# Sorting V as rows in four array tiles, by way of DRAM, for two of four batches of a block-sorted attention with a squared-ReLU MLP

## The chip, the cores and the metric

The kernel runs on one core of one Trainium2 chip. The metric is the device time of one execution in microseconds (us); the profiler's span is the time from the first to the last instruction of the profiled execution.

## The reference

Four batches, eight heads, 768 positions in eight blocks of 96, 64 features per head. A small 8x8 matrix per head, made nearly doubly stochastic by five rounds of normalisation, mixes whole blocks of K and V; each block of Q then attends to one mixed block. The result goes through two dense layers with a squared ReLU between.

```python
P = sort_net                                    # (B, H, 8, 8)
for _ in range(5):
    P = P - np.max(P, axis=-1, keepdims=True)
    P = np.exp(P)
    P = P / (np.sum(P, axis=-1, keepdims=True) + 1e-09)
    P = P / (np.sum(P, axis=-2, keepdims=True) + 1e-09)
k_sorted = np.einsum('bhij,bhjcd->bhicd', P, k_b)
v_sorted = np.einsum('bhij,bhjcd->bhicd', P, v_b)
scores = scale * np.matmul(q_b, k_sb.transpose(0, 1, 2, 4, 3))
attn = softmax(scores)
x = np.matmul(attn, v_sb)                       # -> (3072 tokens, 512)
h = x @ w_in                                    # 512 -> 2048
g = s * np.maximum(h, 0.0) ** 2 + b
out = g @ w_out                                 # 2048 -> 512
```

## The kernel before

All matmuls take bf16 and accumulate in fp32 in PSUM. Work is staged by batch, and each batch by halves of four blocks (384 tokens). The order on every engine is written out by hand: `ffn1` (first dense layer) and `ffn2` (second) each take a dictionary of slots, and pieces of the next batch's attention are called at these slots, between the dense layer's matmuls. So TensorE (PE) works through one fixed list, in order, and waits at whatever comes next on it.

`ffn1` goes over eight pairs of 128 hidden features; ScalarE (ACT) applies the ReLU to a pair and VectorE (DVE) squares it into `gt`. `ffn2` goes over three tiles of 128 tokens with sixteen matmuls each, and its slots count groups of four matmuls. Attention for batch n runs in the two `ffn2` of batch n-1:

- K pieces (`k_piece`, L247): raw K with (head, block, half) in the partitions is the stationary operand, the mixing matrix `PD` the moving one. This sorts K and at once turns it so that features lie in the partitions (`KS`).
- V pieces (`v_piece`, L298): the same with V, but sorted V (`VS`) needs positions in the partitions. So raw V is first permuted by feature into `VP` (GpSimd, POOL, L171, eight copies a batch), and then each of 64 features gets two matmuls of 64 columns: 128 matmuls a batch in four pieces of 32. Each piece is evacuated by ACT or DVE.
- scores with an exponential on ACT (`s_piece`), then P pieces (`p_piece`, L352) that multiply the exponentials with `VS`, whose extra columns of ones give the sums, and a normalisation on DVE.
- the attention result is transposed by DMA (`t_dma`), as Q is (`q_dma`), on the SyncE (SP) queue, which also carries the output stores.

POOL loads K, V and Q by casting DMAs. For batch 1 they follow the weights' loads and some memsets; for batches 2 and 3 they are held back by a gate until the first square of `ffn1` of the batch before them. Raw tiles have two buffers (`rawp`), `VP`, `KS` and `VS` have two each. PSUM has two pools: `psa`, three buffers of two banks, used by `ffn1`, K, V, scores and P; `psb`, two buffers of one bank, used by `ffn2`. Batch 0's attention runs at the start and is not changed but for the name of its mask.

Of the kernel before, what the change touches and what calls it, by code (L numbers as in the profile page):

```python
# [16 lines left out]
def spread(t, dims):  # L17

    return bass.AP(tensor=t.tensor, offset=t.offset, ap=[list(t.ap[0])] + dims)
# [3 lines left out]
def kernel(  # L23
# [26 lines left out]
    KR = GAP + C2  # L50
    NG = NHP * NB
    VW = D + 2
    CK = 16
    scale = float(D) ** -0.5


    raw = [t.rearrange("b h (j z c) d -> b (h j z) (c d)", j=NB, z=2) for t in (q, k, v)]

    const = ctx.enter_context(tc.tile_pool(name="const", bufs=1))
    rawp = ctx.enter_context(tc.tile_pool(name="rawp", bufs=2))  # L60
    trp = ctx.enter_context(tc.tile_pool(name="trp", bufs=2))
    atp = ctx.enter_context(tc.tile_pool(name="atp", bufs=6))
    xp = ctx.enter_context(tc.tile_pool(name="xp", bufs=2))
# [3 lines left out]
    osb = ctx.enter_context(tc.tile_pool(name="osb", bufs=3))  # L67
    psa = ctx.enter_context(tc.tile_pool(name="psa", bufs=3, space=bass.MemoryType.PSUM))
    psb = ctx.enter_context(tc.tile_pool(name="psb", bufs=2, space=bass.MemoryType.PSUM))
    ctx.enter_context(tc.manual_schedule())  # L70


# [11 lines left out]
    def load(t, b, parts=1):  # L84
        ti = rawp.tile([128, C2, D], BF, tag=f"raw{t}", name=f"raw{t}")
        RAW[t, b] = ti
        n = C2 // parts
        for c in range(0, C2, n):
            nc.gpsimd.dma_start(out=ti[:, c:c + n, :].rearrange("p c d -> p (c d)"),
                                in_=raw["qkv".index(t)][b][:, c * D:(c + n) * D])  # L90

    QTOK = {}

    def load_q(b, ns=range(NB)):
# [4 lines left out]
        for n in ns:  # L99
# [2 lines left out]
    zeros = const.tile([128, 512], BF)  # L102
    nc.vector.memset(zeros[:, 0:128], 0.0)  # L103
    nc.vector.memset(zeros[:, 128:512], 0.0)  # L104
    VP = [const.tile([128, D, GAP], BF, name=f"vp{i}") for i in range(2)]
    KS = [const.tile([128, NG, 2, GAP], BF, name=f"ks{i}") for i in range(2)]
    VS = [const.tile([KR, 2 * NG, VW], BF, name=f"vs{i}") for i in range(2)]
    nc.vector.memset(VP[0][:, :, C2:GAP], 0.0)
    nc.vector.memset(KS[0][:, :, :, C2:GAP], 0.0)
    nc.vector.memset(sne[:, NB, :], 1e-9)  # L110

# [3 lines left out]
    idv = ident.rearrange("p (a e j z) -> p a e j z", a=NHP, e=2, j=NB)  # L115
    emat = const.tile([BH, B, 128], FP)
    nc.gpsimd.memset(emat, 0.0)
    nc.gpsimd.affine_select(out=emat, in_=emat, pattern=[[-H, B], [-1, H], [0, 2 * NB]], base=0,
                            channel_multiplier=1, compare_op=ALU.not_equal, fill=1.0)
    load("k", 0, 3)  # L120
    load_q(0, range(HB))
# [24 lines left out]
            fs = slice(c * (NF // 4), (c + 1) * (NF // 4))  # L146
            nc.gpsimd.dma_start(out=wo[:, fs, :], in_=wov[:, fs, :])

    def fill_vs(i):
        nc.gpsimd.memset(VS[i][:, :, D:VW], 1.0)  # L150
        nc.gpsimd.memset(VS[i][32:GAP, :, D:VW], 0.0)
        nc.gpsimd.memset(VS[i][32:C2, :, D:VW], 1.0)

    fill_vs(0)
    Z = []

    def warm(n, w=512):
# [4 lines left out]
                             start=True, stop=True)  # L162


    def permute(eng, b, src, cs=slice(0, C2), ds=slice(0, D)):
        o = VP[b % 2][:, ds, cs]
        i = src[:, cs, ds].rearrange("p c d -> p d c")
        if eng is nc.scalar:
            eng.copy(out=o, in_=i)
        else:  # L170
            eng.tensor_copy(out=o, in_=i)  # L171
# [3 lines left out]
    rrec = const.tile([BH, NB], FP)  # L175
    jsel = const.tile([128, NB], FP)
    bm = const.tile([128, 2 * 2 * NHP], FP)
    idle = [
        lambda: nc.vector.tensor_reduce(
            out=jsel, in_=ident.rearrange("p (h j z) -> p j h z", h=H, j=NB), axis=AX.XY, op=ALU.add),  # L180
# [8 lines left out]
    for it in range(5):  # L189
        nc.scalar.activation(out=sn, in_=sn, func=AF.Exp)  # L190
        if it >= 1:
            permute(nc.scalar, 0, v0f, slice((it - 1) * CV, it * CV))
        if it in (1, 2):
            idle[it - 1]()
        nc.vector.tensor_reduce(out=rstat, in_=sn, axis=AX.X, op=ALU.add)
        nc.vector.reciprocal(out=rrec, in_=rstat)
        nc.vector.tensor_tensor(out=sn, in0=sn, in1=rrec.broadcast_to([BH, NB, NB]), op=ALU.mult)
        if it == 4:
            break
        nc.vector.tensor_reduce(out=rstat, in_=sne.rearrange("p i j -> p j i"),  # L200
                                axis=AX.X, op=ALU.add)
        nc.vector.reciprocal(out=rrec, in_=rstat)
        nc.vector.tensor_tensor(out=sn, in0=sn, in1=spread(rrec, [[0, NB], list(rrec.ap[1])]),
                                op=ALU.mult)
# [11 lines left out]
                             rhs=sn.rearrange("p i j -> p (i j)"), start=True, stop=True)  # L216
        return pe

    def take_p(b0, n, pe):

        bs = slice(b0, b0 + n)
        tmp = rtp.tile([128, n * NB, NB], FP, tag=f"tmp{n}", name="tmp")
        nc.vector.tensor_tensor(out=tmp, in0=pe.rearrange("p b i j -> p (b i) j"),
                                in1=spread(jsel, [[0, n * NB], list(jsel.ap[1])]), op=ALU.mult)
        nc.vector.tensor_reduce(out=PT[:, bs].rearrange("p b i -> p (b i)"), in_=tmp, axis=AX.X,
                                op=ALU.add)
        cs = rtp.tile([128, n], FP, tag=f"cs{n}", name="cs")
        nc.vector.tensor_reduce(out=cs, in_=PT[:, bs], axis=AX.X, op=ALU.add)
        nc.vector.reciprocal(out=RC[:, bs], in_=cs)

    def build_pd(b):
        pd = const.tile([128, 2, 2, NG], BF, name=f"pd{b}")
        nc.vector.scalar_tensor_tensor(
            out=pd.rearrange("p e z (a i) -> p (e z a) i", i=NB),
            in0=spread(bm, [list(bm.ap[1]), [0, NB]]), scalar=RC[:, b:b + 1],
            in1=spread(PT[:, b], [[0, 4 * NHP], list(PT.ap[2])]), op0=ALU.mult, op1=ALU.mult)
        PD[b] = pd

    def evac(eng, out, in_):
        if eng == "A":  # L240
            nc.scalar.copy(out=out, in_=in_)  # L241
        else:
            nc.vector.tensor_copy(out=out, in_=in_)  # L243
# [47 lines left out]
    def q_dma(b):  # L291
        qt = q_tile(b)
        for n0 in (0, HB):
            nc.sync.dma_start_transpose(
                out=qt[:, n0:n0 + HB].rearrange("p n a t -> p (n a) t"),
                in_=QTOK[b][:, n0:n0 + HB].rearrange("p n h d -> p (n h d)"))

    def v_piece(b, d0, eng):  # L298
        ps = psa.tile([128, CK, 2 * NG], FP, tag="a", name="tv")
        for d in range(CK):  # L300
            for z in range(2):
                nc.tensor.matmul(out=ps[z * GAP:(z + 1) * GAP, d, :],  # L302
                                 lhsT=VP[b % 2][:, d0 + d, :], rhs=PD[b][:, :, z, :],
                                 start=True, stop=True)
        evac(eng, VS[b % 2][:, :, d0:d0 + CK], ps[0:KR].rearrange("p d g -> p g d"))

    AT = {}
    X = {}
# [32 lines left out]
    def p_piece(b, half, hp, later=False):  # L341
# [6 lines left out]
        for e in range(2):  # L348
            for n in range(HB):
                c0 = (e * HB + n) * BLK  # L350
                m = 128 if c0 + 128 <= 2 * TG else BLK
                nc.tensor.matmul(out=pv[0:m, e, n * VW:(n + 1) * VW],  # L352
                                 lhsT=atf[:, c0:c0 + m], rhs=VS[b % 2][:, e * NG + g0 + n, :],
                                 start=True, stop=True)

        def norm():
# [100 lines left out]
        nc.sync.dma_start(out=out[r0:r0 + 128, ns], in_=ot[:, ns])  # L457


    take_p(0, 1, spread_p(0, 1))  # L460
    build_pd(0)

    nc.gpsimd.tensor_copy(out=ones[:, 0:1], in_=PD[0][:, 0, 0, 0:1])
# [31 lines left out]
    nc.gpsimd.memset(sel, 0.0)  # L495
    for r in range(0, 128, 32):
        nc.gpsimd.memset(sel[r:r + 1], 1.0)
    nc.gpsimd.memset(VP[1][:, :, C2:GAP], 0.0)
    nc.gpsimd.memset(KS[1][:, :, :, C2:GAP], 0.0)
    fill_vs(1)  # L500
    for t, src in ((s_bc, moe_s), (b_bc, moe_b)):
        nc.gpsimd.dma_start(out=t, in_=src.to_broadcast([128, 1]))

    def v_sort(b):
        for i in range(8):
            permute(nc.gpsimd, b, RAW["v", b], ds=slice(i * 8, (i + 1) * 8))

    def loads(b):
        load("k", b)
        load("v", b)  # L510
        load_q(b)
        v_sort(b)

    loads(1)

# [20 lines left out]

    def K(b, i, eng): return lambda: k_piece(b, i * CK, eng)
    def V(b, i, eng): return lambda: v_piece(b, i * CK, eng)
    def SC(b, h, i): return lambda: s_piece(b, h, i)
    def SB(b, h, i): return lambda: s_banks(b, h, i)  # L540
    def P(b, h, i): return lambda: p_piece(b, h, i)
# [2 lines left out]
    def PDB(b): return lambda: build_pd(b)  # L544
    def QB(b, n0, eng): return lambda: q_blocks(b, n0, eng)
# [2 lines left out]
    ffn1(0, {-1: [TP(0, 0, 2, "AD")], ("pre", 1): [QB(0, HB, "D"), QB(0, HB + 2, "D")],  # L548
             2: [SB(0, 1, 0)], 3: [SB(0, 1, 1), P(0, 1, 0)], 4: [SB(0, 1, 2), P(0, 1, 1)],
             5: [SB(0, 1, 3), P(0, 1, 2)], 6: [TP(0, 1, 0, "D"), P(0, 1, 3)]}, ahead=3)  # L550
    ffn1(1, {-2: [TP(0, 1, 2, "D")], 1: [lambda: take_p(1, B - 1, PB), PDB(1)], 4: [PDB(2)],
             5: [PDB(3), sum_w], 7: [make_bias]}, ahead=3)
    gate = const.tile([128, 1], BF)

    def gated_loads(b):
# [6 lines left out]
    for b in range(B):  # L562
        n = b + 1
        if b:
            ffn1(2 * b, {0: [gated_loads(n)]} if n < B else {})
            ffn1(2 * b + 1, {})
        if n == B:
            ffn2(2 * b, {})
            ffn2(2 * b + 1, {})
            break  # L570
        q_dma(n)
        s0 = {
            2: [K(n, 0, "A"), K(n, 1, "D"), K(n, 2, "A")],
            5: [V(n, 0, "D"), V(n, 1, "A"), V(n, 2, "D")],
            9: [V(n, 3, "D"), SC(n, 0, 0), SC(n, 0, 1)],
            11: [P(n, 0, 0), SC(n, 0, 2), SC(n, 0, 3)]}
        ffn2(2 * b, s0)
        ffn2(2 * b + 1, {0: [P(n, 0, 1)], 1: [P(n, 0, 2)],
                         2: [P(n, 0, 3), TD(n, 0), SC(n, 1, 0), SC(n, 1, 1)],
                         4: [P(n, 1, 0)], 5: [P(n, 1, 1), SC(n, 1, 2), SC(n, 1, 3)],  # L580
                         7: [P(n, 1, 2)], 8: [P(n, 1, 3), TD(n, 1)]})


# [28 lines left out]
```

## Time and profile before

| | us |
|---|---|
| median of 3 runs (lowest, highest) | 229.22 (227.22, 229.44) |
| the profiled execution | 228.41 |
| its span | 226.6 |
| busy in the span: PE, DVE, ACT, POOL | 218.9, 124.5, 99.5, 68.2 |
| sorting V on PE, batches 2 and 3 each (chain of waits) | 1.64 + 0.63 |
| POOL's permutes, a batch (timeline) | 6.3 to 6.4 |

In a row of the page's groups, the line and engine come first, then output and inputs, shapes and count, then busy time and the mean of one, and last the idle time before it with what ended most of it. PE matmuls are pipelined, so the durations of single ones overlap; the chain of waits, which gives start, length and what, tells what a block of them costs. DMA rows give the time from issue to landing.

### The profile page before, as it was taken

To read this page: it belongs to the slowest core of one execution; us is meant where nothing else is said; L and a number is where in the kernel's file an instruction comes from. 1 tells how busy PE (TensorE), PEld (TensorE's weight loads), DVE (VectorE), ACT (ScalarE), POOL (GpSimd) and SP (SyncE) were. 2 spreads that over 40 slices of the span, in tenths; PEclk is the share of its full clock that TensorE was granted. 3 is DMA by queue.
4 is the path that set the end of the run, shared out by engine and by line. 5 is a ranking of instruction groups with operands and counts; after the bars stand their busy time and mean duration, and the time that the engine had idled before them with its cause. 6 is when DMAs were issued, how large, how long until landed. Compare 5 with 4: busy or idle time off the path is not lost.

```text
span 226.6 us, 5806 instructions
## 1 busy us (share of the span) xinstructions
PE 218.9 (97%) x2542; PEld 133.2 (59%) x2542; DVE 124.5 (55%) x223; ACT 99.5 (44%) x128; POOL 68.2 (30%) x112
## 2 busy tenths in 40 slices
PE   7996999999999999999999999999999999999993
PEld 8985656655555556665555556655566566654452
DVE  6766467553647634498656634498557543441121
ACT  4966476564325225637143236627152246550000
POOL 8467797338400009291000028490000000000000
PEclk9999999999999999999999999999999999999999
DMA  5999999999711558993112459991123240001212
GB/s 190 238 105 133 181 164 206 207 196 136 164 49 49 129 151 136 188 166 72 49 47 73 138 120 176 176 171 36 49 95 67 100 114 0 4 0 46 94 49 93
DMA packets 53930, 25.82 MB, mean 114 GB/s; under 512 B 44944, under 2 KB 49296, under 8 KB 53904
## 3 DMA queue, kind: packets, MB, share of 16 engines
q0 software_dynamic: 30864, 12.85, 47.1%
q1 hardware_dynamic: 23040, 12.59, 20.9%
q8 instruction: 20, 0.33, 0.6%
q14 instruction: 6, 0.05, 0.1%
HBM read 27.27 MB, written 6.29 MB: 148 GB/s over the span
## 4 chain that ended last, share of the span: by engine, by line
PE 86%; DVE 5%; DMA 3%; POOL 2%; ACT 1%; issue 1%; POOLq 0%
PE ops L433 36%; PE hps L408 36%; PE pv L352 3%; PE tv L302 3%; DMA qtok<-in_q_dram 3%; PE sc L317 2%; PE tp L252 2%; PE ops L446 2%; POOL wi L131 1%; DMA sne<-in_sort_net_dram 1%; ACT rt L422 1%; POOL qtok L100 1%; ACT sne L190 1%; PE scb L332 1%; DVE rstat L200 0%
## 5 line engine op out<-in xcount | busy, mean ns | idle before, releaser
L408 PE MATMUL hps<-xt,wi 128*128 128x384 bf16 x512 | 85.7, 326 | 0.3 <-DMA qtok<-in_q_dram 0.3
L433 PE MATMUL ops<-wo,gt 128*128 128x512 bf16 x368 | 85.7, 379 | 0.0
L422 ACT ACTIVATE rt<-hps 128x768 bf16<-128x768 f32 x64 | 51.1, 811 | 53.4 <-PE hps L408 45.6
L423 DVE TENSOR_TENSOR gt<-rt 128x768 bf16<-128x768 bf16 x64 | 46.9, 739 | 41.2 <-ACT rt L422 40.4
L408 PEld LDWEIGHTS <-wi 128*128 128x128 bf16 x512 | 49.3, 98 | 33.5 <-issue 0.6
L433 PEld LDWEIGHTS <-gt 128*128 128x128 bf16 x368 | 33.7, 98 | 36.9 <-issue 0.6
L454 DVE SCALAR_TENSOR_TENSOR ot<-ops,s_bc,bias 128x512 f32<-128x512 f32 (+1 forms) x25 | 18.2, 730 | 30.8 <-PE ops L433 28.2
L322 ACT ACTIVATE at<-sc 112x768 bf16<-112x768 f32 x28 | 21.3, 808 | 30.3 <-PE sc L317 30.3
L100 POOL DMA_DIRECT2D qtok<-in_q_dram x32 | 24.9, 793 | 18.4 <-DMA rawv<-in_v_dram 9.0
L360 DVE TENSOR_TENSOR x<-pv,rec 96x512 bf16<-96x512 f32 x32 | 22.0, 687 | 1.1
L243 DVE CAST vs<-tv 112x1024 bf16<-112x1024 f32 x11 | 13.2, 1222 | 10.8 <-PE tv L302 10.7
L171 POOL COPY vp<-rawv 128x384 bf16<-128x384 bf16 x24 | 19.0, 849 | 0.0
L558 POOL COPY gate<-gt 128x1 bf16<-128x1 bf16 x2 | 0.4, 193 | 56.6 <-DVE gt L423 56.6
L352 PEld LDWEIGHTS <-at 112*128 112x128 bf16 (+1 forms) x256 | 12.8, 101 | 7.2 <-ACT at L322 1.1
L352 PE MATMUL pv<-vs,at 112*128 112x66 bf16 (+1 forms) x256 | 13.9, 195 | 1.0 <-DVE vs L243 1.0
L161 PE MATMUL z<-zeros 128*128 128x140 bf16 (+1 forms) x132 | 11.7, 256 | 1.2 <-DVE zeros L104 1.2
L302 PEld LDWEIGHTS <-vp 128*64 128x64 bf16 x512 | 9.0, 113 | 3.9 <-issue 3.6
L161 PEld LDWEIGHTS <-zeros 128*128 128x128 bf16 x132 | 10.1, 111 | 1.4 <-DVE zeros L103 1.0
L302 PE MATMUL tv<-pd,vp 128*64 128x64 bf16 x512 | 10.0, 197 | 0.9 <-issue 0.8
L241 ACT CAST ks<-tp 128x1024 bf16<-128x1024 f32 x8 | 8.1, 1012 | 4.0 <-PE tp L252 3.9
L131 POOL DMA_DIRECT2D wi<-in_moe_w_in_dram x16 | 8.6, 552 | 2.6 <-DMA wi<-in_moe_w_in_dram 0.9
L241 ACT CAST vs<-tv 112x1024 bf16<-112x1024 f32 x5 | 5.1, 1019 | 9.3 <-PE tv L302 9.3
(76 smaller groups left out, 104.3 us busy)
## 6 DMA issues: line engine op xcount, KB each, us to landing
out_dram<-ot SPq DMA_DIRECT2D x23, 256.0 KB, 2.0
qtok<-in_q_dram POOLq DMA_DIRECT2D x32, 96.0 KB, 9.5
rawk<-in_k_dram POOLq DMA_DIRECT2D x3, 768.0 KB, 6.8
rawv<-in_v_dram POOLq DMA_DIRECT2D x3, 768.0 KB, 10.0
wi<-in_moe_w_in_dram POOLq DMA_DIRECT2D x16, 128.0 KB, 5.2
wo<-in_moe_w_out_dram POOLq DMA_DIRECT2D x4, 512.0 KB, 10.8
v0f<-in_v_dram SPq DMA_DIRECT2D x4, 384.0 KB, 4.3
rawk<-in_k_dram POOLq DMA_DIRECT2D x3, 256.0 KB, 7.9
```

Source lines behind the costliest of these rows:

```text
L100: nc.gpsimd.dma_start(out=QTOK[b][:, n], in_=qv[:, n])
L161: nc.tensor.matmul(out=Z[0][:, 0:w], lhsT=zeros[:, 0:128], rhs=zeros[:, 0:w], start=True, stop=True)
L171: eng.tensor_copy(out=o, in_=i)
L302: nc.tensor.matmul(out=ps[z * GAP:(z + 1) * GAP, d, :], lhsT=VP[b % 2][:, d0 + d, :], rhs=PD[b][:, :, z, :], start=True, stop=True)
L322: nc.scalar.activation(out=at, in_=sc[0:KR, :, 0:TG], func=AF.Exp, scale=scale)
L352: nc.tensor.matmul(out=pv[0:m, e, n * VW:(n + 1) * VW], lhsT=atf[:, c0:c0 + m], rhs=VS[b % 2][:, e * NG + g0 + n, :], start=True, stop=True)
L360: nc.vector.tensor_tensor(out=x[:, :, hp * 128:(hp + 1) * 128].rearrange("p n (e d) -> p e n d", e=2), in0=pvv[:, :, :, 0:D], in1=rec.unsq ...
L408: nc.tensor.matmul(out=H1[i][:, f, 0:TG], lhsT=wi[:, hp, fc:fc + 128], rhs=xt[:, :, hp, :], start=(hp == 0), stop=(hp == NHP - 1))
L422: nc.scalar.activation(out=rt, in_=h, func=AF.Relu)
L423: nc.vector.tensor_tensor(out=gt[:, 2 * i:2 * i + 2, :], in0=rt, in1=rt, op=ALU.mult)
L433: nc.tensor.matmul(out=ops, lhsT=gt[:, f, m * 128:(m + 1) * 128], rhs=wo[:, f, :], start=(f == 0), stop=(f == NF - 1))
L454: nc.vector.scalar_tensor_tensor(out=ot[:, ns], in0=ops, scalar=s_bc, in1=BIAS[0][:, ns], op0=ALU.mult, op1=ALU.add)
```

## The change

For batches 2 and 3, V is sorted with the mixing matrix as the stationary operand and raw V as the moving one. Heads are split between the upper and the lower 64 partitions (half z of a block, then head and block), so that the array works as four tiles of 64x64: two halves of the rows (z) and two of the columns (y, even and odd positions). Twelve matmuls of 512 columns a batch replace 128 of 64 columns. The result has (head, block) in the partitions; it is evacuated to `VO`, written by six DMAs on SP to a DRAM tile `DV` in pieces of 96 elements, and read back by two DMAs on POOL into `VS[1]` with positions in the partitions. Columns 64 to 95 of `VO` hold ones. The row matmuls stand in the second `ffn1` of the batch before, after its pairs 3 and 5.

For batch 1, V goes the old way with one `VP`; five eighths of the permute are on POOL and three on DVE. K and V of batches 1 to 3 are loaded in the new partition order, in two DMAs each, with masks of their own. Raw tiles have one buffer. The slots of batches 2 and 3 are laid out anew: scores at slots 7 and 8, P pieces in pairs.

```diff
-    rawp = ctx.enter_context(tc.tile_pool(name="rawp", bufs=2))
+    rawp = ctx.enter_context(tc.tile_pool(name="rawp", bufs=1))
+    drp = ctx.enter_context(tc.tile_pool(name="drp", bufs=1, space=bass.MemoryType.DRAM))
+    def load_z(t, b):
+        ti = rawp.tile([128, C2, D], BF, tag=f"raw{t}", name=f"raw{t}")
+        RAW[t, b] = ti
+        for z in range(2):
+            nc.gpsimd.dma_start(out=ti[z * 64:(z + 1) * 64].rearrange("p c d -> p (c d)"),
+                                in_=rawz["qkv".index(t)][b, z])
-    VP = [const.tile([128, D, GAP], BF, name=f"vp{i}") for i in range(2)]
+    VP = const.tile([128, D, GAP], BF)
-    VS = [const.tile([KR, 2 * NG, VW], BF, name=f"vs{i}") for i in range(2)]
+    VS = [const.tile([KR, 2 * NG, w], BF, name=f"vs{w}") for w in (VW, VR)]
+    DV = drp.tile([BLK, 2 * NG, VR], BF, name="dv")
+    VO = const.tile([128, 2, C2 // 2, VR], BF)
-    nc.gpsimd.affine_select(out=emat, in_=emat, pattern=[[-H, B], [-1, H], [0, 2 * NB]], base=0,
+    nc.gpsimd.affine_select(out=emat[:, 0], in_=emat[:, 0], pattern=[[-1, H], [0, 2 * NB]], base=0,
                             channel_multiplier=1, compare_op=ALU.not_equal, fill=1.0)
...
+    for z in range(2):
+        em = emat[:, 1:B, z * 64:(z + 1) * 64]
+        nc.gpsimd.affine_select(out=em, in_=em, pattern=[[-H, B - 1], [-1, H], [0, NB]], base=-H,
+                                channel_multiplier=1, compare_op=ALU.not_equal, fill=1.0)
...
+    def v_rows(b, i, eng):
+        src, n = RAW["v", b], 8
+        if len(eng) == 1:
+            ps = psa.tile([128, 2, n, D], FP, tag="a", name="vo")
+            ps = [ps[:, z] for z in range(2)]
+        else:
+            ps = [psb.tile([128, n, D], FP, tag="b", name="vob") for _ in range(2)]
+        for y in range(2):
+            for z in range(2):
+                zs, ys = slice(z * 64, (z + 1) * 64), slice(y * 64, (y + 1) * 64)
+                c0 = i * 2 * n + y
+                nc.tensor.matmul(out=ps[z][ys], lhsT=PV[b][zs], rhs=src[zs, c0:c0 + 2 * n - 1:2, :],
+                                 start=True, stop=True, tile_position=(z * 64, y * 64))
+        vo = VO[:, :, i * n:(i + 1) * n, :]
+        for z in range(2):
+            evac(eng[z % len(eng)], vo[:, z, :, 0:D], ps[z])
+        dv = DV.rearrange("(z t c y) g w -> z t (y g) c w", z=2, y=2, c=n)
+        for z in range(2):
+            nc.sync.dma_start(out=dv[z, i], in_=vo[:, z])
+
+    def v_back(b):
+        for z in range(2):
+            nc.gpsimd.dma_start(out=VS[1][z * GAP:z * GAP + C2].rearrange("k g w -> k (g w)"),
+                                in_=DV[z * C2:(z + 1) * C2].rearrange("k g w -> k (g w)"))
...
-    nc.gpsimd.memset(VP[1][:, :, C2:GAP], 0.0)
     nc.gpsimd.memset(KS[1][:, :, :, C2:GAP], 0.0)
-    fill_vs(1)
+    nc.gpsimd.memset(VS[1][32:GAP], 0.0)
+    nc.gpsimd.memset(VO, 1.0)
...
     def loads(b):
-        load("k", b)
-        load("v", b)
+        for t in "kv" if b == 1 else "vk":
+            load_z(t, b)
         load_q(b)
-        v_sort(b)
+        if b == 1:
+            for i in range(5):
+                permute(nc.gpsimd, RAW["v", 1], ds=slice(i * 8, (i + 1) * 8))
...
-    ffn1(1, {-2: [TP(0, 1, 2, "D")], 1: [lambda: take_p(1, B - 1, PB), PDB(1)], 4: [PDB(2)],
-             5: [PDB(3), sum_w], 7: [make_bias]}, ahead=3)
+    ffn1(1, {-2: [TP(0, 1, 2, "D")], 1: [masks_z, lambda: take_p(1, B - 1, PB, jselz), PDB(1)], 4: [PDB(2)],
+             5: [PDB(3), sum_w],
+             7: [make_bias, lambda: permute(nc.vector, RAW["v", 1], ds=slice(40, D))]}, ahead=3)
...
-            ffn1(2 * b + 1, {})
+            ffn1(2 * b + 1, {3: [VR_(n, 0, "AD"), VR_(n, 1, "D")],
+                             5: [VR_(n, 2, "AD"), lambda: v_back(n)]} if n < B else {})
...
+        else:
+            ffn2(2 * b, {2: K3, 7: [SC(n, 0, 0), SC(n, 0, 1)], 8: [SC(n, 0, 2), SC(n, 0, 3)],
+                         10: [P(n, 0, 0), P(n, 0, 1)]})
+            ffn2(2 * b + 1, {0: [P(n, 0, 2), P(n, 0, 3), TD(n, 0)],
+                             1: [SC(n, 1, 0), SC(n, 1, 1)], 2: [SC(n, 1, 2), SC(n, 1, 3)],
+                             4: [P(n, 1, 0), P(n, 1, 1)],
+                             6: [P(n, 1, 2), P(n, 1, 3), TD(n, 1)]})
```

`masks_z` makes the masks for the new partition order on DVE; `build` makes `PD`, and for batches 2 and 3 also `PV`, the mixing matrix as a stationary operand of 64 columns. The slots of batch 1 are as before.

## The prediction

> **What bounds the kernel now.** I read the page first, then the chain of waits in order of time, the groups by form, the timelines of VectorE (DVE), GpSimd (POOL) and SyncE (SP), and stretches of the window view.
>
> ```profile
> span 226.6 us, 5806 instructions
> PE 218.9 (97%) x2542; PEld 133.2 (59%) x2542; DVE 124.5 (55%) x223; ACT 99.5 (44%) x128; POOL 68.2 (30%) x112
> PE 86%; DVE 5%; DMA 3%; POOL 2%; ACT 1%; issue 1%; POOLq 0%
> ```
>
> TensorE (PE) is busy 97% of the span and carries 86% of the chain. So an edit pays if it takes work from PE or makes PE wait. The chain for batch 2, after its two first dense layers:
>
> ```profile
> 102.30 2.59 PE ops L433 x12
> 104.89 1.64 PE tp L252 x96
> 106.53 2.70 PE ops L433 x12
> 109.23 1.64 PE tv L302 x96
> 110.86 3.56 PE ops L433 x16
> 114.42 0.63 PE tv L302 x32
> 115.05 0.45 PE sc L317 x16
> 115.49 1.83 PE ops L433 x8
> ```
>
> Columns: start, length, what. No gap is left between pieces, so here a microsecond off PE is a microsecond off the time. The sorting of V is the two tv rows, 1.64 + 0.63 = 2.27 us per batch. A block of narrow matmuls also costs the full ones behind it: 16 ops take 3.56 where 4 x 0.863 = 3.45 would do, 0.11 more. One row shows four array tiles at work, the column sums of the second weight matrix:
>
> ```profile
> 47.75 0.98 PE cps L527 x16
> 48.73 2.71 PE hps L408 x16
> ```
>
> Sixteen matmuls of 512 columns take 0.98 us, 61 ns each; a lone one takes 216 (2.59/12). So four ran at once: 16 x 216/4 = 0.86 us, and 0.12 for entering. The 16 hps behind take 2.71 against 2.60: 0.11 for leaving.
>
> POOL and DVE, around the permutes of batch 2:
>
> ```profile
> 96.42 6.29 POOL L171 COPY vp<-rawv 128x384 bf16<-128x384 bf16 x8
> 96.68 9.35 DVE L423 TENSOR_TENSOR gt<-rt 128x768 bf16<-128x768 bf16 x6 [0.74 <-ACT rt L422]
> ```
>
> Six squarings that take 0.56 us each elsewhere stretch over 9.35 us while POOL copies, yet PE has no gap there: taking the permutes away wins nothing directly. Two rows for the transfers:
>
> ```profile
> 97.99 1.44 SPq L294 DMA_TRANSPOSE qt<-qtok  x1
> out_dram<-ot SPq DMA_DIRECT2D x23, 256.0 KB, 2.0
> ```
>
> [...]
>
> **The change part by part.**
>
> *V on PE, batches 2 and 3.* Removed: 2.27 us and one exit, 0.11: 2.38. Added: 12 matmuls of 512 columns, 64 rows by 64 columns of the array. Four at once: 3 x 0.216 = 0.65, plus two blocks x (0.12 + 0.11) = 0.46: 1.11. Net 1.27 a batch, 2.54 in all. Bounds: free mode changes give 1.73 a batch (3.5); two at once 6 x 0.216 + 0.46 = 1.76, net 0.62 (1.2); one at a time 3.05, a loss of 0.67 (1.3). The narrow rows already show two at once in either direction (tp: 64 columns at 17 ns each, where 64 columns at 216/512 are 27), and cps shows four, so I take four.
>
> *Evacuations.* Six of 128x512 in place of four of 112x1024, now inside the first dense layer: about 0.6 us each (ACT's copy of cps, same size: 587 ns; half of DVE's 1222 ns). DVE gets four, 2.5 us, ACT two, 1.2 us, per batch. A tile pair of that layer takes PE 1.30, ACT 0.81 and DVE 0.56. With slot 3 ending at T, the borrowed PSUM pair comes free near T + 3.5 and PE wants it for pair 6 near T + 3.7. Cost nothing, cover 0.2 us. [...]
>
> *The way through DRAM.* T is 97.1 (81.5 + 12 x 1.30). Each of six stores has 128 x 8 = 1024 pieces of 192 B: 6144 a batch, 384 for each of 16 DMA engines. SP issues them from T + 1.6 = 98.7; a 128-row store takes SP 0.33 us and a transpose 1.44, so I take 1.0 each, and the last goes out near 104.7. Per piece: while q loads run, pieces of 128 B go at 154 GB/s (98.5 to 99.5), 13 ns per engine; transposes move 256 B pieces at about 220 GB/s, 19 ns. At 13 to 19 ns the data take 5.0 to 7.3 us, plus about 1 us shared with the q loads' tail: done by 104.7 to 107, landed by about 107 to 108 (2.0 us for a store). POOL waits for all six; nothing urgent is behind it. The return, 1.18 MB in rows of 12 KB, I put at 5.5 us from an unloaded K load (6.6 us for 1.57 MB read). VS is then complete at 112.5 to 113.5, up to 1 us later beside the q transposes. The first reader is P(2,0,0): 102.3 + 1.1 (rows) + 2.59 + 1.64 + 4.42 (20 ops) + 0.45 + 0.97 + 0.45 + 1.83 = 115.8. Room about 1 to 3 us; I take no wait. Exhausted when a piece costs more than about 22 ns.
>
> *SP's order.* The six stores stand ahead of the two q transposes, which move from 97.99 and 101.01 to about 105 and 106.5. The first lands 3.8 us after, 109; the first scores, now at slot 7, come at 102.3 + 1.1 + 8.65 = 112.1. Room 3 us: nothing. The out stores behind them are due later.
>
> *Moved slots.* Scores and P pieces go in pairs. PSUM buffers come free in time by 0.81 per exponential and 0.89 per normalisation; the tightest, the second half's second scores, meets its buffer within 0.1 us. The x transposes go out earlier. Nothing.
>
> *Batch 1.* POOL loses a memset of 0.96 and three small ones (0.77), and gains two of 6144 and 4608 columns. At 957 ns per 1024 these are 5.74 + 4.31: loads start 8.3 later, 43.9 for 35.60. In before they queued behind the weights, which landed at 43.8, so most of that was waiting. In batch 2, unloaded, permutes begin 11.6 us after the K issue (84.81 to 96.42): 55.5 here, against 52.90. Five at 0.81 end at 59.6; the V piece that needs the fifth starts near 60.3. Cover 0.7 us. DVE's share, 1152 elements, reaches the queue at 52.9 and waits for V at about 54.6, ahead of POOL, which still issues a q load (0.77). It takes 0.7 to 1.3; behind it stands the K evacuation at 56.05. [...] I take nothing. The masks add about 0.9 us to a DVE with slack. The split of the first mask brings K forward 0.5 us, but the matmuls that use it start at 13.01 on PD: nothing.
>
> **Sum.** 226.6 - 2.5 = 224.1, and the execution lies 1.8 above its span (228.41): 225.9 us, 1.1% under its own before. The three runs' median, 229.22, lies 0.8 higher; against it the same step would read 226.7.
>
> **The rivals.** About 1% is what a measurement of this kernel can tell from no change.
>
> A, as above: 225.9. For it: no gap on PE, and the cps row. Its own range is 224.2 to 227.2.
>
> B, slower: the way through DRAM becomes the wait. Place: P(n,0,0), and before it the first scores, whose q transposes stand behind the stores in the same queue. It decides above about 22 ns a piece and eats the whole gain at 1.3 us late a batch. At 30 ns: 98.7 + 1 + 11.5 + 2 = 113.2, VS at 118.7, 2.9 late, 5.8 in two batches: 226.6 - 2.5 + 5.8 + 1.8 = 231.7. For it: 192 B pieces into DRAM, which nothing here prices; rooms of 1 to 3 us. Against: 128 B pieces at 13 ns into the on-chip memory.
>
> C, no difference: only two array tiles run together, or the return comes about 0.6 us late a batch. 226.6 - 1.2 + 1.8 = 227.2. For it: four tiles that differ in rows and in columns are not in the trace. Against: cps.
>
> **How the numbers follow.** A 0.50 (0.42 faster, 0.08 within 1%), B 0.30 (0.28 slower, 0.02 within), C 0.20 (0.03 faster, 0.15 within, 0.02 slower, where tiles run one by one: 229.8). Together faster 0.45, same 0.25, slower 0.30. Predicted 225.9. The range runs from A's best, 224.2 (1.5 a batch and a little), to B at 231.7.
>
> **What would show it.** Right: a block of 8 row matmuls near 0.55 us and one of 4 near 0.33 in place of 1.64 and 0.63; PE without gaps from 52 us on; the pv matmuls of batches 2 and 3 without a wait. Wrong: PE or its weight loads idle in front of pv for VS, or of sc for qt (B); row blocks of 1 us or more (C); PE waiting for tv or pv in batch 1 near 60 us. B would show in the stores' time to landing, far over 2 us.

## The result, and the profile after

The changed kernel takes 241.0 us (median of 6 runs, 238.3 to 242.35) against 229.08 (6 runs of the kernel before, 227.22 to 229.44): 1.051 times the time before, 95% interval 1.045 to 1.058. It is slower by 5%; 225.9 was forecast. Here and below a ratio leaves out runs more than 1.5% above the fastest of the same kernel, in this case one, while the medians keep them. The profiled execution took 241.5 us. First the same three lines of its page that were read of the kernel before:

```profile
span 239.7 us, 5392 instructions
PE 221.5 (92%) x2310; PEld 130.3 (54%) x2310; DVE 116.7 (49%) x231; ACT 99.5 (42%) x130; POOL 66.9 (28%) x103
PE 74%; DMA 15%; DVE 5%; issue 2%; ACT 2%; POOL 0%; POOLq 0%
```

PE's share of the chain has fallen from 86% to 74%, and transfers hold 15% where they held 3%. PE is also busy 2.6 us longer, although it has 232 matmuls fewer: it must have run slower somewhere. The row of clocks (tenths of full speed in 40 slices of 6 us; all nines before) shows three places, one ahead of the first dense layer, one in batch 2 and one in batch 3:

```profile
PEclk9997999999999999999958999999988999999999
```

The chain of waits for batch 2 (start, length, what; `hps` and `ops` are the matmuls of the first and the second dense layer, `vob` and `vo` the row matmuls, `pv` those of the P pieces) gives the cause:

```profile
98.88 0.34 PE vob L348 x4
99.22 0.22 PE vo L348 x4
99.44 2.71 PE hps L474 x16
102.14 0.34 PE vob L348 x4
...
103.68 4.71 DMA dv<-VO
...
109.97 11.93 DMA vs<-dv
...
122.03 1.09 PE pv L418 x16
123.12 3.41 PE ops L499 x8
```

The row matmuls cost what was forecast, 0.34 + 0.22 and 0.34. The fifth store lands at 103.68 + 4.71 = 108.4 and lets the first half of the return go; the sixth and last lands at 109.4 (104.99 + 4.40). Then the chain stays for 11.93 us in the second half of the return from DRAM, and behind it sixteen pv take 1.09 and eight ops 3.41, about twice the 0.52 and 1.73 that they take elsewhere. In batch 3 the same: `vs<-dv` takes 12.24. TensorE's timeline shows how long it stood, in brackets:

```profile
115.64 1.90 PE L499 MATMUL ops<-wo,gt 128*128 128x512 bf16 x8
122.03 1.09 PE L418 MATMUL pv<-vs,at 112*128 112x66 bf16 x16 [4.49 <-DMA vs<-dv]
```

The list of waits sums this over both batches, 4.5 and 5.4 us (engine, tile, what it waited for, sum, times, longest):

```profile
PE pv L418 <- DMA vs<-dv: 9.9, 2, 5.4
```

The window view, cut around that wait, holds PE's busy time in each stretch, and behind the engines the granted clock:

```profile
118.00:120.00 2.00, 0.00 (x0) 0.00 (x0) 0.00 (x0) 0.00 (x0) 0.00 (x0) 1.00 0.72 115
120.00:121.00 1.00, 0.00 (x0) 0.00 (x0) 0.00 (x0) 0.00 (x0) 0.00 (x0) 0.76 0.73 100
121.00:122.00 1.00, 0.00 (x0) 0.00 (x0) 0.00 (x0) 0.00 (x0) 0.00 (x0) 0.50 1.01 387
...
124.00:126.00 2.00, 2.00 (x6) 0.68 (x5) 1.21 (x2) 0.00 (x0) 0.00 (x0) 0.50 0.00 0
...
127.00:128.00 1.00, 1.00 (x13) 0.60 (x10) 0.93 (x3) 0.00 (x0) 0.00 (x0) 0.83 0.16 62
```

The clock falls to a half at 120.5 us, 3.0 us after the last matmul, and is back at 127.3, 5.3 us after work has come back. In batch 3 it falls at 178.5, 5.2 us after the last matmul, and is back at 182.0, after 3.2 us of work. So each late return costs twice: its wait, and a slow stretch behind it, which is not of one length.

The rows of the transfers show which half of the way failed (KB each, median us from issue to landing):

```profile
dv<-VO SPq DMA_DIRECT2D x12, 192.0 KB, 4.4
vs<-dv POOLq DMA_DIRECT2D x4, 576.0 KB, 10.6
```

One more difference has nothing to do with the return. In this profile the first dense layer starts at 25.87 us, before at 24.09: 1.8 us of the 13.1 between the spans. Over the twelve profiled runs of the changed kernel and its variants below, that start lies anywhere between 23.44 and 26.14, without an edit that touches it (the last variant touches the loads behind it). Part of this is the clock again: in the four latest starts (25.80 to 26.14) it stood at a half for 3.41 us shortly before. In the change that was from 21.53 to 24.94 us, with PE at work throughout, which cost up to half of it, 1.7 us. So spans are best compared from that start on; the last column but one of the table below does that.

### The profile page after: what moved, and what is told of

It is laid out like the page before. It is cut to its first block, busy times and chain, and to the rows that moved or that the text cites. A ratio compares the mean times of both kernels' runs of the same rounds, so it can differ in the third digit from the quotient of the medians.

```text
span 239.7 us, 5392 instructions
## 1 busy us (share of the span) xinstructions
PE 221.5 (92%) x2310; PEld 130.3 (54%) x2310; DVE 116.7 (49%) x231; ACT 99.5 (42%) x130; POOL 66.9 (28%) x103
## 4 chain that ended last, share of the span: by engine, by line
PE 74%; DMA 15%; DVE 5%; issue 2%; ACT 2%; POOL 0%; POOLq 0%
PE hps L474 33%; PE ops L499 27%; DMA vs<-dv 10%; PE pv L418 4%; DMA dv<-VO 4%; PE tv L368 2%; PE sc L383 2%; PE ops L512 1%; PE tp L289 1%; PE z L176 1%; DMA sne<-in_sort_net_dram 1%; ACT rt L488 1%; PE vob L348 1%; ACT sne L207 1%; PE tr L446 1%
## 5 line engine op out<-in xcount | busy, mean ns | idle before, releaser
L499 PE MATMUL ops<-wo,gt 128*128 128x512 bf16 x368 | 87.9, 389 | 0.0
L489 DVE TENSOR_TENSOR gt<-rt 128x768 bf16<-128x768 bf16 x64 | 39.3, 616 | 44.7 <-ACT rt L488 44.5
L499 PEld LDWEIGHTS <-gt 128*128 128x128 bf16 x368 | 34.7, 100 | 39.5 <-issue 3.6
L418 PE MATMUL pv<-vs,at 112*128 112x66 bf16 (+1 forms) x256 | 14.2, 208 | 10.9 <-DMA vs<-dv 9.9
L418 PEld LDWEIGHTS <-at 112*128 112x128 bf16 (+1 forms) x256 | 13.1, 111 | 16.3 <-issue 6.1
L425 DVE RECIPROCAL rec<-pv 96x8 f32<-96x8 f32 x32 | 6.4, 199 | 23.3 <-PE pv L418 23.3
L360 POOL DMA_DIRECT2D vs<-dv x4 | 2.1, 531 | 23.1 <-PE tp L289 11.4
L280 DVE CAST ks<-tp 128x1024 bf16<-128x1024 f32 x4 | 4.9, 1222 | 6.0 <-PE tp L289 6.0
L383 PE MATMUL sc<-qt,ks 64*128 64x96 bf16 x224 | 7.7, 209 | 0.0
L280 DVE CAST vs<-tv 112x1024 bf16<-112x1024 f32 x5 | 6.0, 1218 | 3.4 <-PE tv L368 3.4
## 6 DMA issues: line engine op xcount, KB each, us to landing
vs<-dv POOLq DMA_DIRECT2D x4, 576.0 KB, 10.6
```

The costliest lines, as they stand in the source:

```text
L383: nc.tensor.matmul(out=sc[:, e, n * BLK:(n + 1) * BLK], lhsT=KS[b % 2][pr, g0 + n].rearrange("p z c -> p (z c)"), rhs=QT[b][pr, half * HB ...
L418: nc.tensor.matmul(out=pv[0:m, e, n * VW:(n + 1) * VW], lhsT=atf[:, c0:c0 + m], rhs=VS[b > 1][:, e * NG + g0 + n, 0:VW], start=True, stop= ...
L489: nc.vector.tensor_tensor(out=gt[:, 2 * i:2 * i + 2, :], in0=rt, in1=rt, op=ALU.mult)
L499: nc.tensor.matmul(out=ops, lhsT=gt[:, f, m * 128:(m + 1) * 128], rhs=wo[:, f, :], start=(f == 0), stop=(f == NF - 1))
```

## The experiments

My theory before the experiments: the whole loss is the return, once as a wait and once as the slow clock behind it, and all else in the change gains what was forecast. Of why the return is slow there were two accounts: its destination (48 neighbouring partitions a DMA), called P below, and its source or its way of serving, called S.

| kernel | median us | ratio to before, interval | span | from the first layer's start to the end | PE's wait for VS |
|---|---|---|---|---|---|
| before | 229.08 | | 226.6 | 202.5 | |
| the change | 241.0 | 1.051, 1.045 to 1.058 | 239.7 | 213.8 | 9.9 |
| no return | 226.69 | 0.990, 0.987 to 0.993 | 224.6 | 200.7 | none |
| wide return, not used | 226.11 (one run) | | 224.3 | 199.7 | none |
| two queues | 241.81 | 1.057, 1.052 to 1.062 | 239.8 | 215.2 | 10.9 |
| clock kept up | 236.77 | 1.038, 1.030 to 1.047 | 234.7 | 209.4 | filled, 0.9 left |
| rows early | 242.02 | 1.059, 1.055 to 1.063 | 239.4 | 213.6 | 9.7 |
| 112 partitions | 231.01 | 1.013, 1.008 to 1.017 | 227.9 | 202.8 | 2.7 |
| both | 231.45 | 1.014, 1.009 to 1.019 | 231.4 | 208.0 | 3.4 |
| every second partition | 231.17 | 1.012, 1.006 to 1.019 | 228.3 | 203.2 | 2.9 |
| 112 partitions, P later | 227.33 | 0.994, 0.992 to 0.996 | 225.9 | 199.8 | none |
| only P later | 235.06 | 1.024, 1.017 to 1.030 | 234.3 | 208.5 | 5.6 |
| 112 partitions, P later, fills late | 225.8 | 0.985, 0.981 to 0.990 | 224.0 | 200.2 | 0.2 |

**No return.** `VS[1]` is filled with a constant once, and nothing comes back from DRAM.

```diff
-    nc.gpsimd.memset(VS[1][32:GAP], 0.0)
+    nc.gpsimd.memset(VS[1], 0.5)
...
-        for z in range(2):
-            nc.gpsimd.dma_start(out=VS[1][z * GAP:z * GAP + C2].rearrange("k g w -> k (g w)"),
-                                in_=DV[z * C2:(z + 1) * C2].rearrange("k g w -> k (g w)"))
+        pass
```

> Leaves out the two DMAs per batch that bring V's sorted rows back from DRAM; batches 2 and 3 then multiply with a constant in place of sorted V. Theory 1 (the whole loss of the change is the late return: 4.5 us of wait and about 2.6 us of half clock in each of two batches, and the row matmuls save their 1.27 us a batch as forecast): span 224 to 226.5 us, the row blocks at 0.56 and 0.34 us, no gap in front of pv, clock 0.99 or more. Rival (other parts of the change cost as well, such as the new start or the new slots): a span of 228 us or more, with gaps elsewhere after 30 us.

226.69 us, 0.990 of the kernel before. The clock row is nines throughout, PE is busy 97% as before, and P(2,0,0) stands where it should in the chain:

```profile
114.86 1.83 PE ops L497 x8
116.69 0.52 PE pv L416 x16
```

Batch 2 runs from 82.44 to 131.10 us, 48.66 against 50.01 before (81.50 to 131.51). So the row matmuls, stores, transposes and moved slots together gain 1.35 us a batch, where the prediction had 1.27. The loss of the change, 241.0 - 226.7 = 14.3 us, hangs on the return alone.

**Wide return.** The same bytes come back from `DV`, as one DMA over all 128 partitions, into `VO`, which is not needed any more; nothing waits for them, and P pieces use a constant.

```diff
-        for z in range(2):
-            nc.gpsimd.dma_start(out=VS[1][z * GAP:z * GAP + C2].rearrange("k g w -> k (g w)"),
-                                in_=DV[z * C2:(z + 1) * C2].rearrange("k g w -> k (g w)"))
+        nc.gpsimd.dma_start(out=VO.rearrange("p z c w -> p (z c w)"),
+                            in_=DV.rearrange("k g w -> (k g w)").rearrange("(p x) -> p x", p=128))
...
-    nc.gpsimd.memset(VS[1][32:GAP], 0.0)
+    nc.gpsimd.memset(VS[1], 0.5)
```

> The same 1.18 MB are read back from DRAM on the same queue at the same time, but as one DMA into 128 partitions of a tile that nobody reads; batches 2 and 3 multiply with a constant in place of sorted V. It measures the return's own time. Theory P (the return is slow because each of its DMAs writes 48 neighbouring partitions): 4 to 6 us from issue to landing. Theory S (it is slow because of its source, rows just written in 192 B pieces, or because of the traffic beside it): 9 us or more, as the two DMAs into 48 partitions took.

The page's row of the transfer (KB, median us to landing):

```profile
VO<-dv POOLq DMA_DIRECT2D x2, 1152.0 KB, 7.4
```

Twice the bytes in one DMA land 7.4 us after issue, where each half took 10.6 (medians of two and four; the wide return took 6.3 us in batch 2 and 8.4 in batch 3). The median lies between the two accounts. In batch 2 all bytes are back 6.3 us after issue, and in the change 12.8 us after the first issue. So the source, just written in pieces of 192 B, can't be what makes the return that slow, but both figures are also more than the 5.5 of the prediction.

**Two queues.** The second half of the return goes out on SP, behind the q transposes.

```diff
-    def v_back(b):
-        for z in range(2):
-            nc.gpsimd.dma_start(
+    def v_back(b, zs=(0,)):
+        for z in zs:
+            (nc.sync if z else nc.gpsimd).dma_start(
...
         q_dma(n)
+        if n > 1:
+            v_back(n, (1,))
```

> The second half of the return goes out on SyncE's queue behind the two Q transposes, the first on GpSimd's as before, so that both halves of the partitions are written at once. Theory P (48 neighbouring partitions limit each DMA): VS complete 3 to 5 us sooner, so the wait in front of pv falls from 4.5 to 1.5 us or less and the clock does not halve: 231 to 235 us. Theory S (source or common traffic): VS no sooner, 240 to 242 us.

The chain of waits:

```profile
109.40 12.87 DMA vs<-dv
122.40 1.09 PE pv L419 x16
```

241.81 us: nothing gained. In the records of the DMA engines the 48 rows of POOL's half run from 112.06 to 116.55 us and those of SP's, all but two, from 116.47 to 120.76, so the halves did not run side by side. This run doesn't tell P from S.

**Clock kept up.** Twenty matmuls of 512 columns on zeros, with no use, stand in front of P(n,0,0), so that PE works while it would wait.

```diff
...
-                         10: [P(n, 0, 0), P(n, 0, 1)]})
+                         10: [WM(20), P(n, 0, 0), P(n, 0, 1)]})
```

`WM(20)` calls the helper `warm`, which issues the twenty matmuls.

> Twenty dummy matmuls of 512 columns (4.3 us) stand in front of the first P piece of batches 2 and 3, so TensorE works through most of the wait for VS. Theory 1 (half of what a batch loses after the wait is the clock[...]): the wait stays, filled, the clock stays at 1.00 after it, and 2 to 2.6 us a batch come back: 235 to 237 us. Rival (the clock is a by-product that costs nothing of note): 240 to 242 us.

The chain of waits:

```profile
109.69 11.85 DMA vs<-dv
121.68 0.68 PE pv L418 x16
122.36 1.73 PE ops L499 x8
```

The return is as slow as before, yet the eight ops behind it take 1.73 in place of 3.41. The time falls to 236.77 us, by 4.2. That is the share of the clock, some 2.1 us a batch on average. The clock's own records agree: its half-speed stretches behind the two waits, 120.51 to 127.34 and 178.54 to 181.95 us, hold 5.3 and 3.2 us of work, and half of that is 2.7 + 1.6 = 4.3. The waits are the rest.

**Rows early.** The row matmuls and the return go into slots 0, 1 and 2 of the same `ffn1`, in place of 3 and 5.

```diff
-            ffn1(2 * b + 1, {3: [VR_(n, 0, "AD"), VR_(n, 1, "D")],
-                             5: [VR_(n, 2, "AD"), lambda: v_back(n)]} if n < B else {})
+            ffn1(2 * b + 1, {0: [VR_(n, 0, "AD")], 1: [VR_(n, 1, "D")],
+                             2: [VR_(n, 2, "AD"), lambda: v_back(n)]} if n < B else {})
```

> The row matmuls, their stores to DRAM and the return go out after pairs 0, 1 and 2 of the second first-dense layer in place of 3, 3 and 5, some 4 us sooner; the return itself is as in the change. If the loss is only lateness: VS comes 3 to 4 us sooner, the wait in front of pv falls from 4.5 to about 1 us and the clock does not halve: 230 to 233 us. Rival: the stores of 192 B pieces then run against the loads of K and Q, which fill the DMA engines until about 102 us, and nothing is gained: 239 us or more.

The page's row of the stores (KB, median us to landing), and the chain at the return:

```profile
dv<-VO SPq DMA_DIRECT2D x12, 192.0 KB, 6.7
```

```profile
110.62 11.94 DMA vs<-dv
```

242.02 us, no gain. The stores start 4 us earlier and then run beside the loads of K and Q: a store takes 6.7 us where it took 4.4, and the return starts no earlier.

**112 partitions.** `DV` gets 16 rows of zeros between its halves, so that the return is one DMA over partitions 0 to 111.

```diff
-    DV = drp.tile([BLK, 2 * NG, VR], BF, name="dv")
+    DV = drp.tile([KR, 2 * NG, VR], BF, name="dv")
...
-        for z in range(2):
-            nc.gpsimd.dma_start(out=VS[1][z * GAP:z * GAP + C2].rearrange("k g w -> k (g w)"),
-                                in_=DV[z * C2:(z + 1) * C2].rearrange("k g w -> k (g w)"))
+        nc.gpsimd.dma_start(out=VS[1].rearrange("k g w -> k (g w)"),
+                            in_=DV.rearrange("k g w -> k (g w)"))
...
+    nc.sync.dma_start(out=DV[C2:GAP].rearrange("k g w -> k (g w)"),
+                      in_=VS[1][C2:GAP].rearrange("k g w -> k (g w)"))
```

> The return is one DMA over 112 partitions, both halves and the 16 zero rows between them, in rows of 12 KB as before; the DRAM tile has the 16 zero rows. Theory P (the partitions that the 16 DMA engines write at one time are too near each other: three neighbouring rows each within 48): now seven rows each, spread over 112, go at full rate and land in 6 to 8 us in place of 12; the wait shrinks to 0 to 1 us: 226.5 to 230 us. Theory S (source or traffic): the return has 17% more bytes and takes 13 us or more: 242 us or more.

The page's row of the transfer, and the chain:

```profile
vs<-dv POOLq DMA_DIRECT2D x2, 1344.0 KB, 8.6
```

```profile
109.45 8.08 DMA vs<-dv
117.57 0.69 PE pv L417 x16
118.26 1.73 PE ops L498 x8
```

231.01 us: 10 of the 14.3 are back, with 17% more bytes. The return is complete at 117.5 in place of 121.9; 0.6 us of wait are left in batch 2 and 2.1 in batch 3, and no stretch at half the clock. Both the wait and the time lie above what was expected (0 to 1 us, and 226.5 to 230): in batch 3 the return took 9.1 us.

**Both.** 112 partitions, and the rows early.

> Both together: row matmuls after pairs 0, 1 and 2, and the return as one DMA over 112 partitions. Under theory P the sorted rows are there some 3 us before they are needed and nothing of the way through DRAM is left on the chain: 226 to 227.5 us, 0.985 to 0.995 of the kernel before. Under theory S some wait stays: 232 us or more.

The chain of waits:

```profile
112.46 8.09 DMA vs<-dv
120.59 0.69 PE pv L417 x16
```

231.45 us, no better than with the 112 partitions alone and above the 226 to 227.5 expected, near the rival's 232: the early rows give nothing here either, the wait for VS is 3.4 us in place of 2.7. This run's profile, whose first layer began earliest of all (23.44 us), shows something else in batch 1, in TensorE's timeline:

```profile
59.45 0.44 PE L367 MATMUL tv<-pd,VP 128*64 128x64 bf16 x16 [0.89 <-POOL VP L185]
```

PE waits for POOL's permutes, 2.1 us over five places, none longer than 0.9, and the clock falls to a half all the same, from 61.90 to 65.31 us. One row of the window view (PE's busy time after the stretch's length, the clock third from the end):

```profile
62.00:64.00 2.00, 1.48 (x48) 1.34 (x45) 0.34 (x1) 1.02 (x1) 0.50 (x1) 0.50 1.25 133
```

The last experiment takes these waits up.

**Every second partition.** The two DMAs of 48 rows stay as the change has them, same source, queue and size. Only their destinations differ: partitions 0, 2, ..., 94 and 1, 3, ..., 95. (The zero fill of `VS[1]` at the start covers all its partitions now.)

```diff
-            nc.gpsimd.dma_start(out=VS[1][z * GAP:z * GAP + C2].rearrange("k g w -> k (g w)"),
+            nc.gpsimd.dma_start(out=VS[1][z:2 * C2:2].rearrange("k g w -> k (g w)"),
...
-    nc.gpsimd.memset(VS[1][32:GAP], 0.0)
+    nc.gpsimd.memset(VS[1], 0.0)
```

> The return keeps its two DMAs of 48 rows, its source, its row size, its queue and its order; only the partitions that it writes change: every second one of the first 96, even ones for the first DMA and odd ones for the second, so the rows of V stand in the wrong places for the P pieces, which wait for them as before. Theory P: the two DMAs spread over twice the partitions and land 3 to 5 us sooner: 230 to 236 us. Theory S: nothing moves, 240 to 242 us.

The same two views:

```profile
vs<-dv POOLq DMA_DIRECT2D x4, 576.0 KB, 7.6
```

```profile
109.60 8.11 DMA vs<-dv
117.85 0.68 PE pv L418 x16
```

231.17 us. With nothing changed but which partitions the rows go to, a half lands in 7.6 us in place of 10.6 (medians), and batch 2's second one in 8.11 in place of 11.93. The records of the DMA engines show it row by row: a row of 12,288 B takes 1.31 and 1.37 us in the change (medians of batches 2 and 3), 0.75 and 0.73 here, and 0.60 and 0.59 with the 112 partitions. P holds, and S falls as the reason for this difference.

Side by side, from issue to landing:

| return | us to landing, batches 2 and 3 |
|---|---|
| wide, 128 partitions | 6.3, 8.4 |
| 112 partitions | 8.1, 9.1 |
| every second partition, second half | 8.1, 9.2 |
| as changed, second half | 11.9, 12.2 |

(A second half is counted from its own issue, 0.9 us after that of the first.) Every second partition brought the second half forward by 3.8 and 3.0 us. What stands beside the rows can be read in the DMA records, for batch 2 of the change: 3.7 us pass from the first issue to the first row, 7.8 over all rows, and 1.3 from the last row to landing. With every second partition these are 3.7, 4.6 and 0.7, so 3.2 of the 3.8 us gained lie in the rows themselves. What makes a row slower among neighbouring partitions was not shown. Nor did the two halves run side by side, on two queues (above) or on one: in batch 2 of the change the first 48 rows to start ran from 112.77 to 116.41 us and the other 48 from 116.13 to 120.57. No run here shows why.

**112 partitions, P later.** The P pieces of batches 2 and 3 move three groups back, and the second half's scores with them.

```diff
-            ffn2(2 * b, {2: K3, 7: [SC(n, 0, 0), SC(n, 0, 1)], 8: [SC(n, 0, 2), SC(n, 0, 3)],
-                         10: [P(n, 0, 0), P(n, 0, 1)]})
-            ffn2(2 * b + 1, {0: [P(n, 0, 2), P(n, 0, 3), TD(n, 0)],
-                             1: [SC(n, 1, 0), SC(n, 1, 1)], 2: [SC(n, 1, 2), SC(n, 1, 3)],
-                             4: [P(n, 1, 0), P(n, 1, 1)],
-                             6: [P(n, 1, 2), P(n, 1, 3), TD(n, 1)]})
+            ffn2(2 * b, {2: K3, 7: [SC(n, 0, 0), SC(n, 0, 1)], 8: [SC(n, 0, 2), SC(n, 0, 3)]})
+            ffn2(2 * b + 1, {1: [P(n, 0, 0), P(n, 0, 1)], 2: [P(n, 0, 2), P(n, 0, 3), TD(n, 0)],
+                             3: [SC(n, 1, 0), SC(n, 1, 1)], 4: [SC(n, 1, 2), SC(n, 1, 3)],
+                             6: [P(n, 1, 0), P(n, 1, 1)],
+                             8: [P(n, 1, 2), P(n, 1, 3), TD(n, 1)]})
```

> The return as one DMA over 112 partitions, and the P pieces of batches 2 and 3 three groups (2.6 us) later; the scores of the second half move with them. With 112 partitions alone the P pieces still waited about 0.6 us in batch 2 and 2.1 us in batch 3. My theory (the wait for the return, and the slow clock behind it, are the whole loss): no wait for VS is left, and the time is that of the kernel without the return, 226 to 227.5 us, 0.985 to 0.995 of the kernel before. Rival (the later P pieces only move the wait: x transposes and scores of the second half come late for the next first dense layer, or wait for PSUM): 229 us or more, with a gap of TensorE in front of hps or sc.

The chain of waits:

```profile
116.15 4.26 PE ops L498 x19
120.41 0.52 PE pv L417 x16
120.93 0.86 PE ops L498 x4
```

227.33 us, 0.994 of the kernel before (interval 0.992 to 0.996): faster by 0.6%, with no wait for VS, and pv at its usual 0.52. From the first layer's start to the end it takes 199.8 us, where the prediction's 202.5 - 2.5 would be 200.0.

**Only P later.** The same slots with the return as changed.

> The return as in the change (two DMAs of 48 partitions), and only the P pieces 2.6 us later. The return landed 4.5 us after P(2,0,0) was due, so my theory leaves about 1.9 us of wait a batch[...]: 226.7 + 2 x 1.9 = 230.5 us, 229.5 to 232. If the clock still falls, 233 to 236. Rival (the return is slow because the queue or the engines serve it late, so that it lands with the reader wherever the reader is): about 241 us, as the change.

The list of waits, and the chain:

```profile
PE pv L418 <- DMA vs<-dv: 5.6, 2, 3.2
```

```profile
110.07 13.05 DMA vs<-dv
123.25 0.68 PE pv L418 x16
123.93 0.99 PE ops L499 x4
```

235.06 us: six of the 14.3 are gone. In the expectation's terms the clock still fell in the profiled run, behind waits of 3.2 and 2.4 us: sixteen pv take 0.68, 0.93 and in batch 3 1.12. That run's mean clock was 0.977, at 236.12 us. The quickest run, 232.92 us, had 1.0, so no slow stretch, and lies 5.6 us above the version before, just what the waits come to in the profile. The wait itself, 5.6, is longer than the 3.8 I counted, partly since the return took 13.05 in this execution. The reader's place and the return's length each matter, and neither alone suffices.

**Fills late.** To the version with 112 partitions and later P pieces: POOL's fills of `VS` and `VO`, 5.2 and 3.9 us, which stand ahead of batch 1's loads, move behind batch 1's permutes.

```diff
     nc.gpsimd.memset(KS[1][:, :, :, C2:GAP], 0.0)
-    nc.gpsimd.memset(VS[1][32:GAP], 0.0)
...
-    nc.gpsimd.memset(VO, 1.0)
...
     loads(1)
+    nc.gpsimd.memset(VS[1][32:GAP], 0.0)
...
+    nc.gpsimd.memset(VO, 1.0)
```

> As the version with one return over 112 partitions and later P pieces (227.3 us, 0.994 of the kernel before), and the two GpSimd fills of VS and VO, 5.2 and 3.9 us, moved behind the permutes of batch 1 (the padding rows are then written from GpSimd's queue). Loads of batch 1 start about 36 us in place of 43. My theory: in runs whose first dense layer starts early (23.4 to 24 us) the V piece of batch 1 waits for GpSimd's permutes (0.5 us in the kernel without the return, 2.1 us in the one with both edits); with the loads 7 us earlier that wait goes, and the median falls by 0.3 to 1 us, to 226.3 to 227.0. Rival (the loads land behind the weights whenever they are issued, as in the kernel before, or they delay the weights): no change, 227.0 to 227.7, or slower where the weights come late.

225.8 us, 0.985 of the kernel before (0.981 to 0.990): the fastest version here. POOL's timeline:

```profile
34.18 1.10 POOL L100 DMA_DIRECT2D rawk<-in_k_dram  x2
...
54.53 3.94 POOL L185 COPY VP<-rawv 128x384 bf16<-128x384 bf16 x5
58.54 5.21 POOL L576 MEMSET vs<- 32x6144 bf16 x1
```

The loads start at 34.18 where they started at 42.89 in the change. The permutes start at 54.53, as against 56.67 in the version above, and PE stands nowhere for them, though its first layer began early, at 23.80. Median against median the step gives 1.5 us, more than the 0.3 to 1 that I had written down; the two intervals of the ratio do not meet, but the two were not run together. That the permutes are the reason is not shown: from the first layer's start to the end the two profiles take 200.2 and 199.8 us, and neither waits for them; the one with the fills early merely started late, at 26.14.

## Why the prediction was wrong

**What failed: the return in *The way through DRAM*.** The prediction put it "at 5.5 us from an unloaded K load". It took 12.8 us, from the first issue at 109.05 to 121.9. The K load goes into 128 partitions and was taken as a price per byte; but the return goes into 48 neighbouring ones, twice. Of the 7.3 us that are missing in batch 2, the partitions account for 3.8 (every second partition against the change; 3.0 in batch 3); 0.8 are missing in the wide return too (6.3 to landing; 8.4 in batch 3), 0.9 lie between the two issues, and about 1.8 stay unassigned. One candidate for these was not tested: the 1.57 MB of the K load are bytes read, while 768 KB of it land, and the return lands 1152. So "room about 1 to 3 us" was really a lack of 4.5: the stores landed at 109.4, the return was complete at 121.9, and P(2,0,0) was due at 117.5.

**What was not counted: the clock.** The prediction priced lateness one to one ("2.9 late, 5.8 in two batches"). Measured, the waits are 9.9 us, and the clock adds 4.2 (clock kept up). The sum from the first layer's start: 202.5 - 2.5 + 9.9 + 4.2 = 214.1 against 213.8. The half-speed stretches behind the returns are 6.83 and 3.41 us long, and they begin 3.0 and 5.2 us after the last matmul. With only P later the clock fell 2.1 us after the last matmul, in a wait of 2.4 us; in the run with both edits it fell with no pause over 0.9 us. In that same run a wait of 2.4 us left it at full speed, as waits of 2.1 and 2.2 us did with 112 and with every second partition. So the length of a wait alone doesn't tell what it costs, and what makes the clock fall was not shown.

**Rival B was right in its place and wrong in its cause.** The wait stands at P(n,0,0), as B said. But B priced the pieces of 192 B on the way out, above 22 ns a piece, and the stores were on time: they landed at 109.4, the forecast 107 to 108 plus the later start of 1.8. The median to landing, 4.4 us, was above 2, which the prediction had named as B's sign; it would have led to the wrong half of the way. Had B taken a return of 12.8 us and the clock's 2.1 a batch, it would have stood at 225.9 + 9.9 + 4.2 = 240.0.

**A sum that does not close.** The low end of the range, 224.2, is explained by "1.5 a batch and a little". From the 228.4 us of the profiled execution before, 1.5 a batch leads to 225.4, and the best bound named, 1.73 a batch, to 224.9.

**What held.**
- *V on PE*: 0.56 and 0.34 for the blocks of eight and four (0.55 and 0.33 named): four matmuls of 512 columns take 0.34 us, where a lone one takes 0.216, so four tiles that differ in rows and columns do run at once. (The upper and the lower 64 partitions hold the two halves z of the blocks, with all heads in each; heads are not split between them, as the part on the change has it.) With the return left out, 1.35 us a batch, 1.27 forecast. Rival C falls with it.
- *Evacuations*: no hps waits behind the rows. Without the permutes the squarings keep to 0.56 us each; over the kernel a squaring averages 616 ns, before 739.
- *SP's order*: the stores and then the transposes, as forecast with the later start, and no sc waits for qt; SP's timeline of the change (start, us, what):

```profile
100.23 5.60 SPq L355 DMA_DIRECT2D dv<-VO  x6
106.05 3.94 SPq L331 DMA_TRANSPOSE qt<-qtok  x2
```

- *Moved slots*: no wait in the chains of the versions without the late return.
- *Batch 1*: in the profile after it cost nothing, as forecast: loads at 42.89 (43.9 forecast), permutes from 54.68 to 59.1 (55.5 to 59.6). But its cover of 0.7 us belonged to one start of the first layer. Where that came earlier, PE waited 0.5 us (no return) and 2.1 us (both). With the fills moved out of the way the median was 1.5 us lower, though no profile shows that this came from these waits. "Nothing" should have been a small cost.

What stays open: what else than a slow clock ahead of the four latest moves the first layer's start within 2.7 us, and whether the change moves it on average. Only one profile of the kernel before is at hand, at 24.09.

## What to carry to other kernels

Price a transfer by where it lands as well as by its bytes: two DMAs into 48 neighbouring partitions had everything back 3.0 to 3.8 us later than the same two into every second one, and a single padded DMA, with 17% more bytes, in 8.1 to 9.1 us. A wait on TensorE's path can cost more than its length: behind the change's waits of 4.5 and 5.4 us the slow clock took 4.2 more, behind waits of 2.1 to 2.4 us it took nothing in three profiles and something in a fourth. So where a return may come late, give its reader room of several us, and shorten the return as well where that is not enough: here the shorter return alone left 2.7 us of wait, the later reader alone 5.6, and the two together none. A long fill on the queue that issues loads may be worth moving behind them even where one profile shows it covered; here the time was lower with it, but the cause was not shown.

## What the runs showed of the hardware that was not expected

- Destination partitions set the pace of a return: 7.6 us to landing for every second partition, 10.6 for neighbouring ones (medians), same source, size and queue; one row of 12,288 B took 0.75 and 1.31 us (batch 2).
- Two halves of a return were served one after the other: on one queue the rows ran from 112.77 to 116.41 and from 116.13 to 120.57 us (the change, batch 2), on two from 112.06 to 116.55 and, all but two, from 116.47 to 120.76.
- 6144 pieces of 192 B into DRAM were no hindrance: six stores issued over 5.6 us had landed 9.2 us after the first issue (100.23 to 109.4), and they took 6.7 us each instead of 4.4 when K and Q loads ran beside them.
- TensorE's half-clock stretches behind a wait were 3.41 or 6.83 us long. They began 3.0 and 5.2 us after the last matmul in the change, 2.1 us after it in batch 3 of the run with only P later, and once with no pause over 0.9 us (both).
